# Twelve score pairs in an FFN tile instead of eight, with ten buffers for exponentials and a third residual tile

## The chip, the cores and the metric

The kernel runs on one core of one Trainium2 chip. The metric is device time in microseconds (us) from the first to the last instruction, as the median of several runs; the profile is one further execution with the hardware profiler on. TensorE (PE in the profile) does matmuls, ScalarE (ACT) the exponentials and copies, VectorE (DVE) elementwise work, transposes of 32 x 32 blocks and sums, GpSimd (POOL) casts and adds, SyncE (SP) issues the DMAs.

## The reference

A transformer block on 2048 tokens of width 576, all in float32: pre-normalised multi-query attention with 32 query heads of width 18 that share one key and one value head, then a gated FFN of width 4608 without a nonlinearity.

```python
q = (x @ wq).reshape(B, S, H, Dh).transpose(0, 2, 1, 3)   # S 2048, H 32, Dh 18
k, v = x @ wk, x @ wv
p = softmax(einsum("bhqd,bkd->bhqk", q, k) * Dh ** -0.5)
A = einsum("bhqk,bkd->bhqd", p, v).transpose(0, 2, 1, 3).reshape(B, S, H * Dh) @ wo
h = x0 + A                       # x is layernorm(x0)
n = layernorm(h)
out = h + ((n @ w_gate) * (n @ w_up)) @ w_down
```

## The kernel before, in words

Tokens are worked on in four blocks of 512 (`NB`). Attention of a block goes through 8 groups of four heads (`NG`), each through 16 steps of 128 keys (`NT`). A step is two **pairs**: `pair()` takes a PSUM tile `s` of two banks (two such tiles exist), a buffer `P` for the exponentials (`p_tile`), runs two score matmuls (`scores`, line 596) and one exponential of 128 x 1024 (line 597) from `s` into `P`. So there are 4 x 8 x 16 x 2 = 1024 pairs. `flush()` later turns complete steps into **values** (line 601): four matmuls of 32 columns (two instructions each), which accumulate over the 16 steps of a group in one PSUM bank, `acc`, of which there is one. At a group's end `flush` has VectorE transpose the bank into `os` (line 612). `normalise` divides by the sums and spreads the heads into `ob`; `chunk` and `project` multiply them by `wo` and add the result to the residual `h`. These run from a list, `aux`, of which `run_aux` takes one or two entries in a tile's middle and at its end.

The FFN of a block, `ffn(b)`, has 36 **tiles** of 128 hidden units (`NF`). A tile is 27 steps j of two matmuls each (gate and up, lines 990), then the gate is copied by ScalarE (`g`, line 1020), multiplied by the up half on VectorE (`hf`, line 1024) and made ready for the down product by `left_first` and `left` in odd tiles and `left_sums` in the next even tile (casts on ScalarE, differences on VectorE, line 88 and 89). From the third tile on, every even tile ends with the down product of the two tiles before, `down`, 14 stages of three matmuls (line 950), whose results VectorE adds to `h`, or ScalarE copies to `tmp` (line 957) and GpSimd adds (line 958).

Attention runs ahead inside the FFN: while `more(b + 2)` holds, tiles of block b issue a pair ahead of every fourth step (j = 0, 4, ... 24), and one more after the gate copy: eight in a tile. After `hf` and `left` the tile flushes all its steps at once: this is the tile's **visit** to the values. While pairs run, the gate and up halves use the banks `f` (`pg`, `pu`), otherwise the tile of `s` (`gu`). The last tile of a block has no pairs.

The order on every engine is written out by hand (a manual schedule); semaphores follow from it. Buffers are pools of a fixed number of rooms: a write into a room waits for the last reader of what was there. The exponentials have 6 rooms, from pair 240 on 7. Gate and up weights are loaded into `wr` (two rooms, `load_w`), split into high and low parts by GpSimd and VectorE (`split_w`, at j = 3 of the tile before their use). Residual tiles `h` have two rooms; block b + 2's is loaded at the end of block b's FFN.

Of the kernel before, what the change touches and what calls it, by code (L numbers as in the profile page):

```python
# [17 lines left out]
F32 = mybir.dt.float32  # L18
# [7 lines left out]
P = 128  # L26
# [28 lines left out]
class Block:  # L55
# [509 lines left out]

    def p_tile(self, shape, name):

        i = self.p_next = (self.p_next + 1) % (P_BUFS + (self.p2 is not None and self.n_pair >= P2_FROM))
        pool, tag = (self.pp, "P") if i < P_BUFS else (self.p2, "P2")
        return pool.tile(shape, F32, tag=tag, name=name)  # L570

    def more(self, b):
# [31 lines left out]
    def flush(self, n):  # L604

        for b, g, t, Ps in self.pend[:n]:
            if t == 0:
                self.acc = self.ps_a(f"acc{b}_{g}")
            self.values(self.acc, Ps, t)
            if t == NT - 1:  # L610
                os_ = self.os[g] = self.op.tile([P, TB], F32, tag="os", bufs=1, name=f"os{b}_{g}")
                self.dve.transpose(os_, self.acc)
                if b == 0 and g == NG - 1:
                    self.normalise(b, g, os_)
                else:
                    self.aux.insert(len(self.aux) if b else 0, (self.round + 1, lambda b=b, g=g, o=os_: self.normalise(b, g, o), None))
        del self.pend[:n]

    def run_aux(self, limit=1, within=False):
# [78 lines left out]
    def chunk_of(self, b, c):  # L698
        to = self.heads_to(b, c)
        (self.split_tail if b and c == 4 else self.split)(*to, self.ob[0:rows(b, c), c])  # L700


    def load_wo(self, c):
# [12 lines left out]

    def load_wo_0(self, c):

        r = self.wo_r0[c] = self.w0.tile([P, D], F32, tag="wo_r", bufs=3, name=f"wo_r{c}")
        self.sp.dma_start(r, self.wo0[:, c])  # L720

    def split_wo_0(self):

        self.wo_0 = self.wp.tile([P, 2, 5, D], F32R, tag="X", bufs=1, name="wo_0")
        for c in range(3):
            if c not in self.wo_r0:
                self.load_wo_0(c)
        for c in range(5):
            self.split(self.wo_0[:, 0, c], self.wo_0[:, 1, c], self.wo_r0.pop(c), self.nc.gpsimd.tensor_copy)
            self.wo_in.add(c)  # L730
            if 0 < c < 3:
                self.load_wo_0(c + 2)
            yield
            if c == 2:
                yield
# [114 lines left out]
    def load_w(self, n):  # L850

        if n < NF * NB:
            r = self.wr[n] = self.wp.tile([P, 9, P], F32, tag="wr", bufs=2, name=f"wr{n}")
            self.sp.dma_start(r, self.wgu[n % NF])

    def split_w(self, n):
        if n < NF * NB:
            r = self.wr.pop(n)
            w = self.ws[n] = self.wp.tile([P, 2, 9, P], F32R, tag="ws", bufs=2, name=f"ws{n}")
            self.split(w[:, 0], w[:, 1], r, self.nc.gpsimd.tensor_copy)  # L860
            self.load_w(n + 2)

    def load_wd(self, n):

# [31 lines left out]
    def down(self, b, pair):  # L896

        pe, dve, act, sp, pool = self.pe, self.dve, self.act, self.sp, self.nc.gpsimd
        h = self.h[b]
        W = [self.wdo.pop((b, pair, j), None) for j in range(7)]  # L900
        if pair == NC - 1:
            ys = {}

            def part(s, n, i):

                ms = [(self.A[:, k, 2 * i + s // 2], W[(1, 0, 2, 3)[2 * i + n]][:, l]) for k, l in ((0, 0), (0, 1), (1, 0))]
                for j, (m, k) in enumerate(ms):
                    pe.matmul(ys[s, n][:, :HD], m[:, s % 2 * P:(s % 2 + 1) * P], k, start=(i == j == 0), stop=(i == 1 and j == 2))  # L908

            if b == NB - 1:  # L910
                e = self.ps_s("ye")
                for k, y in enumerate((e[:, 0], e[:, 1], self.ps_f("ye2"), self.ps_f("ye3"), self.ps_m("ye4"), self.ps_a("ye5"))):
                    ys[k // 2, k % 2] = y
                    part(k // 2, k % 2, 0)
            def add(s, n):
                hs, y = h[:, s, n * HD:(n + 1) * HD], ys.pop((s, n))[:, :HD]
                if b < NB - 1 and n:
                    z = self.tmp[:, self.n_tmp % 5]
                    self.n_tmp += 1
                    act.copy(z, y)  # L920
                    pool.tensor_tensor(hs, hs, z, ALU.add)
                else:
                    dve.tensor_tensor(hs, hs, y, ALU.add)

            for s in range(NQ):
                for n in range(2):
                    if (s, n) not in ys:
                        if b < NB - 1:
                            ys[s, n] = self.ps_y(2 * s + n, f"y{b}_{pair}_{s}_{n}")
                        else:  # L930
                            e = self.ps_s("ye6") if n == 0 else e
                            ys[s, n] = e[:, n]
                        part(s, n, 0)
                    part(s, n, 1)
                    if b < NB - 1:
                        add(s, n)
                        yield
                if b == NB - 1:
                    for n in range(2):
                        add(s, n)  # L940
                    yield
                sp.dma_start(self.tokens(self.out, b)[:, s], h[:, s, :])
            return
        c, a = self.ps_f(f"y{b}_{pair}_2"), self.ps_f(f"y{b}_{pair}_0")
        banks = [a, self.ps_m(f"y{b}_{pair}_1"), c]
        for i, (t, bank, (x, w), first, (s, n), on_dve) in enumerate(STAGES):
            y = banks[bank]
            ms = [(self.A[:, k, x], W[w][:, l]) for k, l in ((0, 0), (0, 1), (1, 0))]
            for j, (m, k) in enumerate(ms):
                pe.matmul(y[:, :HD], m[:, t * P:(t + 1) * P], k, start=(first and j == 0), stop=(j == 2), skip_group_check=True)  # L950
            hs = h[:, t + 2 * s, n * HD:(n + 1) * HD]
            if on_dve:
                dve.tensor_tensor(hs, hs, y[:, :HD], ALU.add)  # L953
            else:
                z = self.tmp[:, self.n_tmp % 5]
                self.n_tmp += 1
                act.copy(z, y[:, :HD])  # L957
                pool.tensor_tensor(hs, hs, z, ALU.add)  # L958
            yield

    def room(self):
# [2 lines left out]
        self.A = e[:, 0:14 * HT].rearrange("p (k n q) -> p k n q", k=2, n=7)  # L964
        self.o_hl = e[:, 14 * HT:].rearrange("p (k q) -> p k q", k=2)
        self.S = self.hh.tile([P, 4, HT], F32, tag="S", bufs=1, name="S")
        self.tmp = self.hh.tile([P, 5, HD], F32, tag="tmp", bufs=1, name="tmp")
        self.n_tmp = 0

    def ffn(self, b):  # L970
        pe, act, dve = self.pe, self.act, self.dve
        X, hid, todo = self.X, [], None
        for f in range(NF):
# [10 lines left out]
            j = 0  # L984
            for c in range(9):
                for wk, xk in ((0, 0), (0, 1), (1, 0)):
                    if on and not last and j % 4 == 0 and self.more(b + 2):
                        self.pair()
                    for o, ps in ((0, pg), (64, pu)):
                        pe.matmul(ps, w[o:o + 64, wk, c], X[o:o + 64, xk, c], start=(j == 0), stop=(j == 26))  # L990
# [46 lines left out]
        if b + 1 < NB:  # L1037
            both(self.spread(b + 1), self.down(b, *todo))
            self.more_wd(b + 1, WD_BUFS if b == 0 and self.first else 4)
            if b + 2 < NB:  # L1040
                self.load_x(b + 2)
        else:
            drain(self.down(b, *todo))

    def load_x(self, b):
        h = self.h[b] = self.hp.tile([P, NQ, D], F32, tag="h", name=f"h{b}")
        self.sp.dma_start(h, self.tokens(self.x, b))

    def fill(self, time, keep=2):
# [61 lines left out]
    def begin(self, first):  # L1111
# [3 lines left out]
        self.n_wd = 0  # L1115
        self.os, self.h, self.qt, self.normed, self.wr, self.ws, self.wdo, self.wo_r, self.wos = ({} for _ in range(9))
        self.n_pair, self.half, self.pend, self.aux, self.round = 0, [], [], [], 0
        self.p_next, self.wo_r0, self.wo_in, self.yos, self.n_yo, self.due, self.odd = -1, {}, set(), [], 0, 0.0, 0

    def blocks(self):  # L1120

        work = self.split_wo_0()
        next(work)
        self.load_w(0)
        self.load_w(1)
        self.cast = self.dve.tensor_copy
        self.steps(lambda: len(self.wo_in) < 5, work)
        drain(work)
# [23 lines left out]
        if self.first:  # L1152
            self.load_raw(0)
        else:
            self.load_wd(WD_BUFS)
        for b in range(NB):
            self.ffn(b)
        del self.A, self.o_hl, self.S, self.tmp, self.X, self.ob, self.mv

    def run(self):  # L1160
# [3 lines left out]
        self.wd_dram = tc.dram_tile([NC, P, 7, 2, HD], F32, name="wd_dram")  # L1164
        self.m_dram = tc.dram_tile([NB, 2, H, TB], F32, name="m_dram")
        self.known, self.n_mx = [0] * NB, 0
        self.tqs, self.p2 = [], None
        self.begin(True)
        with ExitStack() as st:
            pool = lambda name, bufs, **k: st.enter_context(tc.tile_pool(name=name, bufs=bufs, **k))  # L1170
            cp, self.lp, self.hp = pool("const", 1), pool("ln", 2), pool("resid", 2)
            self.qp, self.pp, self.op, self.otp = pool("q", 2), pool("P", P_BUFS), pool("o", 1), pool("oT", 1)
            self.ps, self.w0 = pool("ps", 1, space=PSUM), pool("w0", 3)
            self.C = cp.tile([P, C_W], F32, name="C")
            self.ident = self.C[:, C_ID:C_ID + P]
            self.kT = cp.tile([P, S], F32R, name="kT")
# [4 lines left out]
            with tc.tile_pool(name="p0q", bufs=1) as self.p0q:  # L1181
# [4 lines left out]
                with tc.tile_pool(name="qb", bufs=2) as self.qb:  # L1186
# [6 lines left out]
                    live, due = True, 0.0  # L1193
                    while live:
                        if self.n_pair >= WO_FROM and not self.wo_r0:
                            for c in range(3):
                                self.load_wo_0(c)
                        self.pair()
                        due += RATE
# [4 lines left out]
                        self.pair()  # L1204
                        self.run_aux(1)
                        self.flush(len(self.pend) - 1)
            self.wp, self.hh, self.p2 = pool("w", 2), pool("hid", 4), pool("P2", 1)
            self.blocks()
            self.guard()

# [11 lines left out]
LANDING = 12  # L1222
WO_FROM = 200
YO = 10
P2_FROM = 240
STAGES = [(0, 0, P1, True, (0, 0), True), (1, 1, P1, True, (0, 0), True), (0, 2, P5, True, (1, 1), False),
          (0, 0, P6, False, (0, 1), True), (1, 1, P6, False, (0, 1), False), (0, 2, P3, False, (0, 1), False),
          (0, 0, P7, False, (1, 1), False), (1, 1, P7, False, (1, 1), True), (1, 2, P5, True, (1, 1), False),
# [123 lines left out]
```

## Time and profile before

| | |
|---|---|
| median of 3 runs | 2287.27 us (2287.25 to 2287.45) |
| span of the profiled execution | 2285.5 us |
| first FFN matmul | 359.8 us into the span |
| mean granted TensorE clock | 1.000 |
| DMA, mean over the span | 134 GB/s |

A row of the profile's groups and lines reads: source line, engine, operation, output<-inputs, their shapes, count | busy us, mean ns of one | idle time of the engine ahead of them and what ended it. A row of the timeline reads: start in us from the span's start, duration in us, engine, line, operation, output<-inputs, shapes, count of merged instructions, and in brackets the idle time ahead of it and its releaser. A row of the windows reads: window, its length, busy time and count of each engine, granted clock, DMA share, GB/s. Ends of matmuls are modelled, their starts are not; the argument goes by starts.

### The profile page before, as it was taken

Reading aid. Unit: us, or ns where it says so; the run is one execution under the profiler, and the core shown is the slowest. Engines: PE = TensorE matmul, PEld = TensorE weight load, DVE = VectorE, ACT = ScalarE, POOL = GpSimd, SP = SyncE. Lnnn points to the kernel's source line nnn. Section 1 sums busy time; section 2 is a strip of 40 time slices with the busy share of each in tenths; the row PEclk is TensorE's granted clock in tenths of the full one; section 3 lists DMA queues with packets and bytes.
Section 4 is the critical chain, followed back from the end, with each engine's and each line's share of the span. In section 5 each row is a group of like instructions: output and inputs, shape, how many; then the busy total and the mean of one; then the engine's idle time right before and its main releaser. Section 6 shows DMA issues by size and latency. Waiting matters only on the chain.

```text
span 2285.5 us, 45923 instructions
## 1 busy us (share of the span) xinstructions
PE 2264.4 (99%) x18114; PEld 1610.0 (70%) x18114; DVE 1183.9 (52%) x2152; ACT 1438.0 (63%) x1877; POOL 683.1 (30%) x856
## 2 busy tenths in 40 slices
PE   8999999999999999999999999999999999999998
PEld 6433345677777667677767777777767788898887
DVE  8332435565656566343434455444444476566565
ACT  5899887777676676767666767667677623232332
POOL 4000002455554444122221222222122233333332
PEclk9999999999999999999999999999999999999999
DMA  5222314444333444633333443643333355655553
GB/s 174 75 79 72 117 30 136 144 143 147 134 123 129 141 159 135 210 114 123 113 113 108 126 129 125 193 126 120 100 120 116 122 172 174 212 172 172 179 185 112
DMA packets 127129, 306.75 MB, mean 134 GB/s; under 512 B 17553, under 2 KB 17681, under 8 KB 126265
## 3 DMA queue, kind: packets, MB, share of 16 engines
q1 hardware_dynamic: 126905, 303.73, 40.6%
q8 instruction: 145, 2.38, 0.4%
q14 instruction: 79, 0.65, 0.1%
HBM read 233.76 MB, written 55.67 MB: 127 GB/s over the span
## 4 chain that ended last, share of the span: by engine, by line
PE 95%; DVE 2%; DMA 1%; ACT 1%; issue 0%; SPq 0%; POOL 0%; DVEq 0%; ACTq 0%; POOLq 0%
PE pg L990 21%; PE acc L601 20%; PE y L950 17%; PE gu L990 13%; PE s L596 12%; PE pu L990 5%; PE yo L754 3%; PE psq L448 2%; PE y L908 1%; DMA X<-X 1%; PE psk L236 0%; DVE XT L89 0%; PE ye L908 0%; DVE bsa L103 0%; ACT P L597 0%
## 5 line engine op out<-in xcount | busy, mean ns | idle before, releaser
L597 ACT ACTIVATE P<-s 128x1024 f32<-128x1024 f32 x1024 | 1025.4, 1027 | 263.6 <-PE s L596 187.1
L990 PE MATMUL pg<-X,ws 64*128 64x512 f32 x2592 | 702.6, 389 | 0.1
L990 PE MATMUL pu<-X,ws 64*128 64x512 f32 x2592 | 702.5, 389 | 0.1
L990 PEld LDWEIGHTS pg<-X,ws 64*128 64x128 f32 x2592 | 479.4, 185 | 69.2 <-issue 1.2
L990 PEld LDWEIGHTS pu<-X,ws 64*128 64x128 f32 x2592 | 477.3, 185 | 15.2 <-DVE h L755 1.0
L601 PE MATMUL acc<-P,V 128*32 128x512 f32 x4096 | 487.9, 598 | 0.0
L596 PE MATMUL s<-q,kT 56*128 56x512 f32 x2048 | 452.6, 421 | 3.6 <-DVE XT L89 1.8
L950 PEld LDWEIGHTS y<-wdo,room 128*128 128x128 f32 x2856 | 386.1, 188 | 47.6 <-issue 44.2
L950 PE MATMUL y<-wdo,room 128*128 128x288 f32 x2856 | 403.6, 300 | 0.1
L957 ACT COPY tmp<-y 128x288 f32<-128x288 f32 x408 | 162.9, 400 | 331.0 <-PE y L950 313.5
L596 PEld LDWEIGHTS s<-q,kT 56*128 56x128 f32 x2048 | 210.4, 184 | 188.7 <-ACT P L597 106.9
L990 PE MATMUL gu<-X,ws 64*128 64x512 f32 x2592 | 301.7, 389 | 0.6 <-DMA X<-X 0.6
L958 POOL TENSOR_TENSOR x<-x,tmp 128x288 f32<-128x288 f32 x204 | 159.1, 808 | 440.7 <-ACT tmp L957 439.8
L601 PEld LDWEIGHTS acc<-P,V 128*32 128x32 f32 x4096 | 113.9, 109 | 241.6 <-issue 230.6
L990 PEld LDWEIGHTS gu<-X,ws 64*128 64x128 f32 x2592 | 250.1, 184 | 46.3 <-issue 4.7
L88 POOL CAST ws<-wr 128x1152 fp32r<-128x1152 f32 x144 | 171.4, 1190 | 321.8 <-PE pu L990 173.5
L958 POOL TENSOR_TENSOR h<-h,tmp 128x288 f32<-128x288 f32 x204 | 159.0, 810 | 345.4 <-ACT tmp L957 345.1
L89 DVE TENSOR_TENSOR ws<-wr,ws 128x1152 fp32r<-128x1152 f32 x144 | 199.8, 1387 | 75.4 <-POOL ws L88 75.4
L1024 DVE TENSOR_TENSOR hf<-pu,g 128x512 f32<-128x512 f32 x96 | 66.3, 691 | 265.3 <-ACT g L1020 258.6
L953 DVE TENSOR_TENSOR x<-x,y 128x288 f32<-128x288 f32 x272 | 117.4, 453 | 145.5 <-PE y L950 145.5
L953 DVE TENSOR_TENSOR h<-h,y 128x288 f32<-128x288 f32 x272 | 118.1, 454 | 112.0 <-PE y L950 108.9
L89 DVE TENSOR_TENSOR room<-S,room 128x1024 fp32r<-128x1024 f32 x68 | 85.5, 1257 | 144.3 <-ACT room L88 144.3
(172 smaller groups left out, 1630.2 us busy)
## 6 DMA issues: line engine op xcount, KB each, us to landing
wdo<-wd_dram SPq DMA_DIRECT2D x369, 288.0 KB
wr<-in_wgu_dram SPq DMA_DIRECT2D x144, 576.0 KB
wd_dram<-wdo SPq DMA_DIRECT2D x123, 288.0 KB
q<-q_dram SPq DMA_DIRECT2D x64, 216.0 KB
raw<-in_wd_dram SPq DMA_DIRECT2D x36, 288.0 KB
q_dram<-qs SPq DMA_DIRECT2D x15, 504.0 KB
X<-X SPq DMA_DIRECT2D x24, 256.0 KB
ob<-ob SPq DMA_DIRECT2D x121, 36.0 KB
```

What stands on the lines that cost most here:

```text
L88: (copy or self.cast)(hi, src)
L89: self.dve.tensor_tensor(lo, src, f32(hi), ALU.subtract)
L596: self.pe.matmul(s_[:, i], self.kT[o:o + 56, t * P:(t + 1) * P], q[o:o + 56, pr], start=True, stop=True)
L597: self.act.activation(p_, s_, AF.Exp, scale=SCALE)
L601: self.pe.matmul(acc[32 * j:32 * j + 32, :], self.V[:, t, :], Ps[j // 2][:, j % 2, :], start=(t == 0), stop=(t == NT - 1), skip_group_chec ...
L754: pe.matmul(y[:, :HD], m, k, start=(i == 0), stop=(i == len(ms) - 1))
L950: pe.matmul(y[:, :HD], m[:, t * P:(t + 1) * P], k, start=(first and j == 0), stop=(j == 2), skip_group_check=True)
L953: dve.tensor_tensor(hs, hs, y[:, :HD], ALU.add)
L957: act.copy(z, y[:, :HD])
L958: pool.tensor_tensor(hs, hs, z, ALU.add)
L990: pe.matmul(ps, w[o:o + 64, wk, c], X[o:o + 64, xk, c], start=(j == 0), stop=(j == 26))
L1024: dve.tensor_tensor(hf, pu, g, ALU.mult)
```

## The change

- The exponentials get ten rooms: the 6, two in a pool `early` (which holds the raw `wo` chunks first, two at a time instead of three) and two in a pool `late`. All ten are used once the five `wo` chunks are in (`len(self.wo_in) == 5`).
- `SPOTS` replaces every fourth step: eleven places in a tile, and the one after the gate copy as before, so twelve pairs. The visit is still one, at the same place, now for six steps.
- Block 2's residual tile has a room of its own (`hp2`), loaded ahead of block 0's FFN; block 3's is loaded after block 0's.
- To make space, `wr` has one room instead of two (`load_w(n + 1)` after the split of tile n's weights, `load_w(1)` at the start goes) and `tmp` four instead of five.
- `normalise` of a block's first group waits, for blocks 2 and 3, until the block before has its last chunk split out of `ob` (`split_to`).

```diff
@@ p_tile
-        i = self.p_next = (self.p_next + 1) % (P_BUFS + (self.p2 is not None and self.n_pair >= P2_FROM))
-        pool, tag = (self.pp, "P") if i < P_BUFS else (self.p2, "P2")
+        i = self.p_next = (self.p_next + 1) % (P_BUFS + (EARLY + LATE if len(self.wo_in) == 5 else 0))
+        pool, tag = (self.pp, "P") if i < P_BUFS else (self.early, "P2") if i < P_BUFS + EARLY else (self.late, "P3")
@@ flush
-                    self.aux.insert(len(self.aux) if b else 0, (self.round + 1, lambda b=b, g=g, o=os_: self.normalise(b, g, o), None))
+                    free = (lambda b=b: self.split_to >= b) if g == 0 and b > 1 else None
+                    self.aux.insert(len(self.aux) if b else 0, (self.round + 1, lambda b=b, g=g, o=os_: self.normalise(b, g, o), free))
@@ chunk_of
+        if c == 4:
+            self.split_to = b + 1
@@ load_wo_0, split_wo_0
-        r = self.wo_r0[c] = self.w0.tile([P, D], F32, tag="wo_r", bufs=3, name=f"wo_r{c}")
+        r = self.wo_r0[c] = self.early.tile([P, D], F32, tag="P2", name=f"wo_r{c}")
...
-            if 0 < c < 3:
-                self.load_wo_0(c + 2)
+            if c + EARLY < 5:
+                self.load_wo_0(c + EARLY)
@@ load_w, split_w
-            r = self.wr[n] = self.wp.tile([P, 9, P], F32, tag="wr", bufs=2, name=f"wr{n}")
+            r = self.wr[n] = self.wp.tile([P, 9, P], F32, tag="wr", bufs=1, name=f"wr{n}")
...
-            self.load_w(n + 2)
+            self.load_w(n + 1)
@@ down (twice), room
-                    z = self.tmp[:, self.n_tmp % 5]
+                    z = self.tmp[:, self.n_tmp % N_TMP]
...
-        self.tmp = self.hh.tile([P, 5, HD], F32, tag="tmp", bufs=1, name="tmp")
+        self.tmp = self.hh.tile([P, N_TMP, HD], F32, tag="tmp", bufs=1, name="tmp")
@@ ffn
-                    if on and not last and j % 4 == 0 and self.more(b + 2):
+                    if on and not last and j in SPOTS and self.more(b + 2):
                         self.pair()
...
-            if b + 2 < NB:
-                self.load_x(b + 2)
+            if b == 0:
+                self.load_x(3)
@@ load_x
-        h = self.h[b] = self.hp.tile([P, NQ, D], F32, tag="h", name=f"h{b}")
+        pool, tag = (self.hp2, "h2") if b == 2 else (self.hp, "h")
+        h = self.h[b] = pool.tile([P, NQ, D], F32, tag=tag, name=f"h{b}")
@@ blocks
-        self.load_w(1)
...
+        self.load_x(2)
         for b in range(NB):
             self.ffn(b)
@@ run
-            self.ps, self.w0 = pool("ps", 1, space=PSUM), pool("w0", 3)
+            self.ps, self.early = pool("ps", 1, space=PSUM), pool("P2", EARLY)
...
-            self.wp, self.hh, self.p2 = pool("w", 2), pool("hid", 4), pool("P2", 1)
+            self.wp, self.hh, self.late, self.hp2 = pool("w", 2), pool("hid", 4), pool("P3", LATE), pool("resid2", 1)
@@ constants
-P2_FROM = 240
+EARLY, LATE = 2, 2
+N_TMP = 4
+SPOTS = (0, 1, 4, 7, 10, 12, 15, 18, 21, 24, 26)
```

More of the change, by code (lines that the diff above doesn't have):

```diff
@@ L724, in split_wo_0 @@
         self.wo_0 = self.wp.tile([P, 2, 5, D], F32R, tag="X", bufs=1, name="wo_0")
-        for c in range(3):
+        for c in range(EARLY):
             if c not in self.wo_r0:
@@ L954, in down @@
             else:
-                z = self.tmp[:, self.n_tmp % 5]
+                z = self.tmp[:, self.n_tmp % N_TMP]
                 self.n_tmp += 1
@@ L1117, in begin @@
         self.n_pair, self.half, self.pend, self.aux, self.round = 0, [], [], [], 0
-        self.p_next, self.wo_r0, self.wo_in, self.yos, self.n_yo, self.due, self.odd = -1, {}, set(), [], 0, 0.0, 0
+        self.p_next, self.wo_r0, self.wo_in, self.yos, self.n_yo, self.due, self.odd, self.split_to = -1, {}, set(), [], 0, 0.0, 0, 0
     def blocks(self):
@@ L1166, in run @@
         self.known, self.n_mx = [0] * NB, 0
-        self.tqs, self.p2 = [], None
+        self.tqs = []
         self.begin(True)
@@ L1195, in run @@
                         if self.n_pair >= WO_FROM and not self.wo_r0:
-                            for c in range(3):
+                            for c in range(EARLY):
                                 self.load_wo_0(c)
```

## The prediction

> **What bounds the kernel now.** I read the page first: busy shares, slices and chain.
>
> ```profile
> PE 2264.4 (99%) x18114; PEld 1610.0 (70%) x18114; DVE 1183.9 (52%) x2152; ACT 1438.0 (63%) x1877; POOL 683.1 (30%) x856
> ACT  5899887777676676767666767667677623232332
> PE 95%; DVE 2%; DMA 1%; ACT 1%; issue 0%; SPq 0%; POOL 0%; DVEq 0%; ACTq 0%; POOLq 0%
> L597 ACT ACTIVATE P<-s 128x1024 f32<-128x1024 f32 x1024 | 1025.4, 1027 | 263.6 <-PE s L596 187.1
> ```
>
> TensorE is the bound everywhere: 99% busy and 95% of the chain. ScalarE is at six to seven tenths while exponentials run, then at two to three. So a change gains only where it shortens TensorE's own stream, and loses wherever it makes TensorE wait. Next, the groups by line, those of the exponentials up to the first FFN tile (a window that ends at 359.9 us) and those of the gate copies:
>
> ```profile
> L597 ACT ACTIVATE P<-s 128x1024 f32<-128x1024 f32 x272 | 263.4, 1023 | 38.6 <-PE s L596 38.0
> ...
> L1020 ACT COPY g<-pg 128x512 f32<-128x512 f32 x96 | 55.7, 580 | 5.6 <-PE pg L990 5.6
> L1020 ACT COPY g<-gu 128x512 f32<-128x512 f32 x48 | 28.3, 590 | 117.3 <-PE gu L990 117.3
> ```
>
> 272 of the 1024 pairs are done before the FFN, 752 inside it. At eight a tile that is 94 tiles; two more tiles (the last of blocks 0 and 1) use the same banks without pairs, which makes the 96. The other 48 are plain. At twelve a tile the 752 pairs need 62 tiles and one with eight: 35 in block 0 (272 + 420 = 692, under the limit of 768 that `more(2)` sets), 27 and the short one in block 1. So the change can do what it says.
>
> Then the timeline of TensorE, around an odd and an even tile of block 0 and a plain two-tile period of block 3:
>
> ```profile
> 688.31 0.50 PE L596 MATMUL s<-q,kT 56*128 56x512 f32 x2
> ...
> 706.07 0.50 PE L596 MATMUL s<-q,kT 56*128 56x512 f32 x2
> ...
> 707.32 0.41 PE L596 MATMUL s<-q,kT 56*128 56x512 f32 x2
> 707.55 0.39 PE L990 MATMUL pg<-X,ws 64*128 64x512 f32 x1
> ...
> 713.98 0.41 PE L596 MATMUL s<-q,kT 56*128 56x512 f32 x2
> 714.32 3.64 PE L601 MATMUL acc<-P,V 128*32 128x512 f32 x32
> 717.89 0.50 PE L596 MATMUL s<-q,kT 56*128 56x512 f32 x2
> ...
> 725.92 0.39 PE L596 MATMUL s<-q,kT 56*128 56x512 f32 x2
> 726.24 1.06 PE L601 MATMUL acc<-P,V 128*32 128x512 f32 x8
> ...
> 1972.54 0.73 PE L990 MATMUL gu<-X,ws 64*128 64x512 f32 x4
> ...
> 1990.85 0.73 PE L990 MATMUL gu<-X,ws 64*128 64x512 f32 x4
> ```
>
> Even tile (with its down product) 706.07 - 688.31 = 17.76, odd tile 717.89 - 706.07 = 11.82: 29.58 for two tiles with 16 pairs. A plain two tiles take 1990.85 - 1972.54 = 18.31. Sixteen pairs therefore cost 11.27. A score step takes 707.55 - 707.32 = 0.23, and the values of one step (two pairs, 8 instructions) (3.64 - 1.06) / 3 = 0.86.
>
> **What it removes: visits.** A tile with four more pairs and no waiting is longer by 4 x 0.23 + 2 x 0.86 = 2.64. The even tile's last scores come 725.92 - 717.89 = 8.03 after its first, the odd one's 713.98 - 706.07 = 7.91: 0.12 is lost to waiting today. Without it, two tiles of twelve take 29.58 - 0.12 + 5.28 = 34.74. Today the same weights and 24 pairs take 18.31 + 1.5 x 11.27 = 35.22. The gain is 0.48 per two tiles, over 31.3 such periods 15 us. The Trainium skill (TensorEngine Tiling (Array Packing), Key Properties) says that a change of tiling mode drains TensorE, and each visit is such a change, which speaks for the change; the 15 us hold that drain already.
>
> **What it adds, first: ScalarE's pace.** Scores still have two PSUM buffers, so scores i wait until exponential i - 2 has been read. In the program's order FFN matmuls and values stand behind waiting scores on the same engine. The rows of ScalarE:
>
> ```profile
> 348.20 2.85 ACT L597 ACTIVATE P<-s 128x1024 f32<-128x1024 f32 x3
> ...
> 706.61 2.19 ACT L597 ACTIVATE P<-s 128x1024 f32<-128x1024 f32 x2
> 708.69 0.40 ACT L88 CAST room<-hf 128x256 fp32r<-128x256 f32 x1
> 708.99 5.54 ACT L597 ACTIVATE P<-s 128x1024 f32<-128x1024 f32 x5
> 714.43 0.58 ACT L1020 COPY g<-pg 128x512 f32<-128x512 f32 x1
> 715.48 1.02 ACT L597 ACTIVATE P<-s 128x1024 f32<-128x1024 f32 x1 [0.47 <-PE acc L601]
> ...
> 721.71 1.04 ACT L88 CAST room<-S 128x1024 fp32r<-128x1024 f32 x1
> 722.64 2.85 ACT L597 ACTIVATE P<-s 128x1024 f32<-128x1024 f32 x3
> ...
> 849.45 1.03 ACT L597 ACTIVATE P<-s 128x1024 f32<-128x1024 f32 x1
> ...
> 850.53 0.50 PE L596 MATMUL s<-q,kT 56*128 56x512 f32 x2
> ```
>
> The first exponential starts 706.61 - 706.07 = 0.54 after its scores. Back to back, three take 2.85, so one follows another by (2.85 - 1.03) / 2 = 0.91. Scores that wait go 850.53 - (849.45 + 1.03) = 0.05 after the exponential ends. The twelfth scores need the tenth exponential: 0.54 + 9 x 0.91 + 1.03 + 0.05 = 9.81 after the tile's start at the earliest. TensorE alone would be there at 7.91 + 4 x 0.23 = 8.83. It waits 0.98. The new spots, three FFN steps apart, just match 0.91; the two gaps of two steps and the pair after the last matmul do not. Other ScalarE work inside the tile adds in full, since nothing covers it any more: in odd tiles `left_first`, 708.99 - 708.69 = 0.30, in even ones `left_sums`, 722.64 - 721.71 = 0.93. So 1.28 in an odd tile, 1.91 in an even one. There are 30 of each and two block starts without that work: 38 + 57 + 2 = **97 us**. The Trainium skill (ScalarE: Activation LUTs, What ACT_TABLE_LOAD costs) gives an ACTIVATE with immediate operands 186 ns plus 0.833 ns an element, less 93 ns back to back: an estimate of 0.95 for 1024, against 0.91 in this trace. By that page the waiting would be 0.3 longer per tile, about 20 us in all.
>
> **What it adds, second: groups end inside a visit.** 16 steps make a group of heads, which accumulates in one PSUM bank, `acc`. At its end VectorE transposes the bank into `os`, and the next group's values wait for that. 136 steps are done before the FFN, 8 past a group's end. Today's visits of four steps end with every group, so nothing stands behind the transpose for a tile. Visits of six put the ends after 2, 0 and 4 steps in turn. By the tile count, of the 24 group ends in the FFN 15 fall inside a visit: after two steps in 5 odd tiles (1, 9, 17, 25, 33 of block 0) and 3 even (6, 14, 22 of block 1); after four steps in 4 even (6, 14, 22, 30 of block 0) and 3 odd (3, 11, 19 of block 1). Rows of VectorE:
>
> ```profile
> L612 DVE STREAM_TRANSPOSE os<-acc 128x512 f32<-128x512 f32 x24 | 17.2, 718 | 21.4 <-PE acc L601 19.8
> ...
> 93.08 0.72 DVE L612 STREAM_TRANSPOSE os<-acc 128x512 f32<-128x512 f32 x1 [12.61 <-PE acc L601]
> ...
> 94.09 0.64 PE L601 MATMUL acc<-P,V 128*32 128x512 f32 x4
> ...
> 1084.94 0.69 DVE L1024 TENSOR_TENSOR hf<-pu,g 128x512 f32<-128x512 f32 x1 [3.56 <-ACT g L1020]
> ...
> 1087.24 0.68 DVE L89 TENSOR_TENSOR room<-hf,room 128x512 fp32r<-128x512 f32 x1
> ```
>
> In program order `hf`, and in odd tiles `left`, come before the transpose. Count from the visit's start. With ten rooms, exponential 11 waits for the first step's values, as the eighth does today: 715.48 - 714.32 = 1.16. The gate copy is queued behind it, 0.91 later at 2.07, and takes 0.58. `hf` runs from 2.68 to 3.37, the transpose to about 4.1; in odd tiles `left` ends 1087.92 - 1084.94 = 2.98 after `hf` began, at 5.66, the transpose at 6.3. From its end to the next values lies between 0.05 (the wait for ScalarE above) and 0.29 (94.09 - 93.80); I take 0.1, nearest to a wait that really held TensorE. TensorE is ready at 1.72 after two steps, 3.44 after four. It waits 4.7 and 3.0 in odd tiles, 2.5 and 0.8 in even: 5 x 4.7 + 3 x 3.0 + 3 x 2.5 + 4 x 0.8 = **43 us**. Nothing else can hide this: behind `acc` all of TensorE stands.
>
> **What I cost at nothing.**
>
> ```profile
> 702.26 4.80 POOL L958 TENSOR_TENSOR x<-x,tmp 128x288 f32<-128x288 f32 x6 [8.82 <-ACT tmp L957]
> ...
> 704.21 0.40 ACT L957 COPY tmp<-y 128x288 f32<-128x288 f32 x1 [0.40 <-PE y L950]
> ...
> 1975.90 10.01 SPq L854 DMA_DIRECT2D wr<-in_wgu_dram  x2
> ...
> 1984.21 1.35 DVE L89 TENSOR_TENSOR ws<-wr,ws 128x1152 fp32r<-128x1152 f32 x1
> ...
> 1972.50:1990.85 18.35, 18.35 (x153) 16.36 (x152) 11.12 (x20) 5.58 (x12) 6.88 (x9) 1.00 0.52 177
> ...
> PE gu L990 <- DMA X<-X: 0.6, 1, 0.6
> ```
>
> Four `tmp` instead of five: the fifth copy (704.21) needs the first add, done at 702.26 + 0.80 = 703.06; 1.1 to spare, and up to 0.8 a down product if POOL starts late. One `wr` instead of two: SP waits for the same VectorE split as now, so nothing more stands behind it; a load issued at 1975.90, in a plain stretch, now feeds the next split, whose VectorE half comes at 1984.21. 576 KB at the window's 177 GB/s are 3.3 us, the cast 1.2: hidden by 3.8; beyond that each plain tile would be late by the excess. Block 2's residual, 1152 KB, moves ahead of block 0: 6.7 us of DMA behind the raw weights on SP's queue, for data used a block later; nothing to 7 once. Two early loads instead of three: nothing to 3.3 (two of 288 KB), under the steps of pairs. Block 2 now starts without pairs over its X moves; block 3's start lost 0.6 so: +1.
>
> **Sum.** 2285.5 - 15 + 97 + 43 + 1 = 2411.5 for the profiled execution; the median of the runs stands 1.8 above its span: **2413**.
>
> **Rivals.**
> - *ScalarE's pace alone* (the transposes find VectorE free early, or the ends fall elsewhere): without the 43, 2370. For it: VectorE is half idle. Against: `hf` itself hangs on the delayed exponential.
> - *More than both*: the chunk casts of `ob` (0.6) fall inside waiting tiles, and the four `tmp` hold ScalarE for one 0.8 add in each of 31 down products: up to 30 on top, 2443. For it: nothing on ScalarE is covered any more. Against: 1.1 us to spare.
> - *Faster*: the exponentials keep up and only the visits go: 2413 - 97 - 43 = 2273. It decides where an exponential follows another by (8.83 - 0.54 - 1.03 - 0.05) / 9 = 0.80 or less and groups end with visits; the row says 0.91. The skill's drain rule, above, is the argument for it.
> - *It does not do what it says* (pairs stop at the limit and spill into block 2): against it the count above; 2287.
>
> **How the numbers follow.** Forecast 0.6, pace alone 0.18, more than both 0.15, faster 0.04, no change 0.03. The range goes from just under the pace alone (2366) to the third case (2443). A measurement here tells 0.2% from no change, 4.6 us. Faster 0.04, same 0.03, slower 0.93.
>
> **What would show it.** Right: TensorE's waits list scores behind `P` L597 with about a hundred us, and `acc` behind `os` L612 with some forty in 15 places; twelve-pair tiles near 15.8 (odd) and 22.1 (even). Wrong: such tiles near 14.5 and 20.3, or exponentials less than 0.85 apart, or `acc` never late.

## The result, and the profile after

| | before | after |
|---|---|---|
| median of the runs | 2287.36 us (2287.25 to 2287.78) | 2449.62 us (2446.42 to 2452.95) |
| ratio, 95% interval | | 1.0709 [1.0694, 1.0724] |
| span of the profiled execution | 2285.5 us | 2444.6 us |
| mean granted TensorE clock | 1.000 | 0.994 |

The change makes the kernel 7.1% slower. The forecast was 2413 with a range up to 2443: the side is right, and the time lies 6.6 us above the range. First the page of the changed kernel: span, busy shares, the chain by engine and by line, and two groups.

```profile
span 2444.6 us, 45830 instructions
...
PE 2339.9 (96%) x18114; PEld 1572.9 (64%) x18114; DVE 1194.4 (49%) x2152; ACT 1396.7 (57%) x1877; POOL 675.3 (28%) x856
...
PE 62%; ACT 24%; DVE 7%; issue 4%; DMA 1%; SPq 0%; POOL 0%; ACTq 0%; DVEq 0%; POOLq 0%
...
L597 ACT ACTIVATE P<-s 128x1024 f32<-128x1024 f32 x1024 | 982.8, 1045 | 298.9 <-PE s L596 198.2
L601 PE MATMUL acc<-P,V 128*32 128x512 f32 x4096 | 492.6, 606 | 39.3 <-DVE os L612 39.3
```

TensorE has the same 18114 instructions as before, but its share of the chain went from 95% to 62%: ScalarE now holds 24% and VectorE 7%. These are the two engines that TensorE waits for. TensorE's busy time rose too, by 75 us (2264.4 to 2339.9), though the work is the same; some of that is waiting that the modelled ends count as busy, and some is a slower clock, below.

**Scores wait for exponentials.** TensorE's waits in the changed kernel (us in total, times, longest), and its timeline through an odd and an even tile of twelve pairs:

```profile
PE acc L601 <- DVE os L612: 39.3, 15, 4.3
PE s L596 <- ACT P L597: 38.2, 120, 0.9
```

```profile
1613.51 0.50 PE L596 MATMUL s<-q,kT 56*128 56x512 f32 x2
...
1623.70 0.50 PE L596 MATMUL s<-q,kT 56*128 56x512 f32 x2 [0.18 <-ACT P L597]
1624.13 5.36 PE L601 MATMUL acc<-P,V 128*32 128x512 f32 x48
1629.42 0.50 PE L596 MATMUL s<-q,kT 56*128 56x512 f32 x2
...
1635.70 0.50 PE L596 MATMUL s<-q,kT 56*128 56x512 f32 x2 [0.67 <-ACT P L597]
...
1640.28 0.50 PE L596 MATMUL s<-q,kT 56*128 56x512 f32 x2 [0.19 <-ACT P L597]
...
1651.82 0.51 PE L596 MATMUL s<-q,kT 56*128 56x512 f32 x2
```

The last scores start 10.19 after the first in the odd tile and 10.86 in the even one; the prediction had 8.83 + 1.28 = 10.11 and 8.83 + 1.91 = 10.74. The tiles take 15.91 and 22.40 (predicted near 15.8 and 22.1). The row of waits shows only 38.2 us for this, since many waiting scores are put down with no idle time ahead of them. So I took the starts of all score matmuls: first to last of each tile, less what TensorE alone needs (7.91 for eight pairs, 0.23 more for each further one). Summed over the tiles with pairs that is 107.9 us, against 11.6 in the kernel before.

**A group's end inside a visit.** Tile 9 of block 0, in the timelines of TensorE and VectorE:

```profile
548.97 1.92 PE L601 MATMUL acc<-P,V 128*32 128x512 f32 x16
555.23 5.15 PE L601 MATMUL acc<-P,V 128*32 128x512 f32 x32 [4.33 <-DVE os L612]
...
551.66 0.69 DVE L1027 TENSOR_TENSOR hf<-pu,g 128x512 f32<-128x512 f32 x1 [4.66 <-ACT g L1023]
...
553.86 0.69 DVE L89 TENSOR_TENSOR room<-hf,room 128x512 fp32r<-128x512 f32 x1
554.46 0.71 DVE L612 STREAM_TRANSPOSE os<-acc 128x512 f32<-128x512 f32 x1
```

After two steps (16 instructions) TensorE waits 4.33 us. VectorE was idle for 4.66, waiting for the gate copy, and had the transpose queued behind `hf` and `left`. This is the predicted order, and the predicted 15 places: 4.33 where 4.7 was predicted.

**The clock halves after such a wait.** The windows of the changed kernel (window, length, busy time and count of PE, PEld, DVE, ACT, POOL, then the granted clock):

```profile
554.90:558.30 3.40, 3.07 (x16) 0.79 (x20) 1.51 (x2) 0.00 (x0) 2.42 (x3) 0.50 0.35 96
...
1172.73:1176.14 3.41, 1.27 (x12) 0.42 (x16) 3.33 (x6) 0.00 (x0) 0.00 (x0) 1.00 0.00 0
1176.14:1179.55 3.41, 3.41 (x20) 1.84 (x14) 0.00 (x0) 1.41 (x2) 0.00 (x0) 0.50 0.54 173
...
1394.60:1398.01 3.41, 1.47 (x16) 0.55 (x20) 1.31 (x2) 1.47 (x3) 0.00 (x0) 1.00 0.00 0
1398.01:1401.42 3.41, 3.41 (x34) 1.70 (x22) 0.61 (x2) 0.00 (x0) 0.00 (x0) 1.00 0.00 0
```

Right behind the wait of 4.33 TensorE runs at half clock for 3.4 us: 16 to 20 instructions in a window that holds 34 at full clock. The trace has eight such spells ahead of the kernel's end (the kernel before has none): after all five waits of 4.33, after two of the three waits of 2.6, and one at a block's start (2114.8). A spell does half of 3.4 us of work, so it costs 1.7 us; eight cost about 13.6.

**The plain tiles are slower as well.** Tiles 3 to 34 of block 3 have no pairs, the same work in both kernels. (A plain tile here is one without pairs that is not the last of its block; in even tiles it holds the down product.) The windows over that stretch, of the kernel before and of the changed one:

```profile
1972.54:2265.67 293.13, 293.12 (x2401) 258.61 (x2400) 177.14 (x305) 88.88 (x177) 110.66 (x129) 1.00 0.51 173
```

```profile
2127.83:2424.96 297.13, 295.58 (x2401) 258.44 (x2400) 182.90 (x305) 88.88 (x177) 110.97 (x129) 1.00 0.51 172
```

and from the groups by line in it one row each of VectorE and GpSimd, again before and after:

```profile
L887 DVE TENSOR_TENSOR S<-hf,hf 128x256 f32<-128x256 f32 x16 | 6.8, 425 | 0.5
...
L88 POOL CAST ws<-wr 128x1152 fp32r<-128x1152 f32 x32 | 36.9, 1153 | 71.4 <-PE gu L990 71.4
```

```profile
L890 DVE TENSOR_TENSOR S<-hf,hf 128x256 f32<-128x256 f32 x16 | 13.3, 834 | 0.5
...
L88 POOL CAST ws<-wr 128x1152 fp32r<-128x1152 f32 x32 | 37.2, 1162 | 84.9 <-DMA wr<-in_wgu_dram 84.9
```

The stretch takes 4.0 us more, at full clock. GpSimd's cast of the raw weights used to wait for TensorE, now for the load of `wr`. And an addition on VectorE takes twice as long, 834 ns instead of 425. The timelines of one even tile of the changed kernel (GpSimd, VectorE, TensorE), and of one of the kernel before, show how the two hang together:

```profile
1959.07 1.16 POOL L88 CAST ws<-wr 128x1152 fp32r<-128x1152 f32 x1 [5.50 <-DMA wr<-in_wgu_dram]
1959.38 1.11 DVE L890 TENSOR_TENSOR S<-hf,hf 128x256 f32<-128x256 f32 x1
...
1963.89 1.35 DVE L89 TENSOR_TENSOR ws<-wr,ws 128x1152 fp32r<-128x1152 f32 x1
1965.16 0.81 DVE L956 TENSOR_TENSOR h<-h,y 128x288 f32<-128x288 f32 x2
...
1965.66 4.73 PE L953 MATMUL y<-wdo,room 128*128 128x288 f32 x33 [0.22 <-DVE h L956]
```

```profile
1997.33 1.15 POOL L88 CAST ws<-wr 128x1152 fp32r<-128x1152 f32 x1 [4.45 <-PE gu L990]
...
1998.70 0.43 DVE L887 TENSOR_TENSOR S<-hf,hf 128x256 f32<-128x256 f32 x1
...
2002.52 1.35 DVE L89 TENSOR_TENSOR ws<-wr,ws 128x1152 fp32r<-128x1152 f32 x1
```

Before, the cast is over (1998.48) when VectorE starts its addition. After, the cast comes later, because the load does, and lies on top of the addition, which ends 0.26 after the cast (1960.49 and 1960.23). All that is queued behind it on VectorE is 0.7 late: its half of the split, and behind that the sums of the down product, whose PSUM buffers TensorE waits for. The Trainium skill (SBUF — State Buffer, Who interferes with whom) says that a VectorE instruction with two inputs in SBUF contends with a GpSimd instruction that reads SBUF, since they share a pair of ports under an exclusive lock. The trace agrees: 1.11 instead of 0.43, ended 0.26 after the cast.

At the start of blocks 2 and 3 the late load costs TensorE directly. The row of waits of the changed kernel has two entries that the kernel before does not have:

```profile
PE gu L993 <- POOL ws L88: 1.9, 2, 0.9
PE gu L993 <- DVE ws L89: 1.3, 2, 0.7
```

In tile 2 of each of these blocks TensorE waits for both halves of the split itself (from 1768.05 and from 2112.15 on). In block 2 the room comes free at 1758.51, when VectorE has done its half of the split before; the load is issued at 1761.28, behind stores of results and loads of `wdo` on SyncE's queue, and the cast starts at 1767.79. The spell of half clock at 2114.8 follows the waits in block 3.

Tile by tile the span's +159.1 us comes apart like this:

| | predicted | measured |
|---|---|---|
| scores late (107.9 - 11.6); the 97, less 0.12 in 31 periods today | +93 | +96.3 |
| values wait for `os`, 15 places | +43 | +39.3 |
| half clock, seven spells in tiles with pairs | 0 | about +12 |
| plain tiles (excess 21.5 - 2.3, with the spell at 2114.8) | +1 | +19 |
| fewer visits, without those 0.12, and all else (what is left over) | -11 | -7.5 |

The excess of the plain tiles is their time over 6.25 us (odd), 12.06 (even, with its down product) and the output projections in them, summed over all of them. The kernel before has 46 plain tiles, the changed one 77. About 11 us of it lie in the 36 even tiles behind a block's start, 0.3 each, and most of the rest in the first three tiles of blocks 2 and 3. The profiled execution was the quickest of the four; their median stands 3.2 above it.

### The profile page after: what moved, and what is told of

Its sections match the earlier page's. It is cut to its first block, busy times and chain, and to the rows that moved or that the text cites. A ratio compares the mean times of both kernels' runs of the same rounds, so it can differ in the third digit from the quotient of the medians.

```text
span 2444.6 us, 45830 instructions
## 1 busy us (share of the span) xinstructions
PE 2339.9 (96%) x18114; PEld 1572.9 (64%) x18114; DVE 1194.4 (49%) x2152; ACT 1396.7 (57%) x1877; POOL 675.3 (28%) x856
## 4 chain that ended last, share of the span: by engine, by line
PE 62%; ACT 24%; DVE 7%; issue 4%; DMA 1%; SPq 0%; POOL 0%; ACTq 0%; DVEq 0%; POOLq 0%
ACT P L597 21%; PE acc L601 19%; PE y L953 15%; PE gu L993 15%; PE s L596 6%; PE yo L757 3%; ACT room L88 2%; PE psq L448 1%; DVE ws L89 1%; DVE hf L1027 1%; DVE S L890 1%; ACT g L1023 1%; PE pg L993 1%; DVE S L891 1%; DMA wr<-in_wgu_dram 1%
## 5 line engine op out<-in xcount | busy, mean ns | idle before, releaser
L597 ACT ACTIVATE P<-s 128x1024 f32<-128x1024 f32 x1024 | 982.8, 1045 | 298.9 <-PE s L596 198.2
L601 PE MATMUL acc<-P,V 128*32 128x512 f32 x4096 | 492.6, 606 | 39.3 <-DVE os L612 39.3
L993 PE MATMUL pu<-X,ws 64*128 64x512 f32 x1728 | 516.6, 394 | 0.0
L993 PE MATMUL pg<-X,ws 64*128 64x512 f32 x1728 | 515.8, 394 | 0.0
L993 PE MATMUL gu<-X,ws 64*128 64x512 f32 x4320 | 506.2, 390 | 3.5 <-POOL ws L88 1.9
L596 PE MATMUL s<-q,kT 56*128 56x512 f32 x2048 | 465.5, 445 | 41.3 <-ACT P L597 38.2
L993 PEld LDWEIGHTS gu<-X,ws 64*128 64x128 f32 x4320 | 414.8, 185 | 84.9 <-issue 7.4
L596 PEld LDWEIGHTS s<-q,kT 56*128 56x128 f32 x2048 | 195.4, 184 | 327.5 <-ACT P L597 247.0
L993 PEld LDWEIGHTS pg<-X,ws 64*128 64x128 f32 x1728 | 323.0, 187 | 42.8 <-issue 1.0
L961 POOL TENSOR_TENSOR x<-x,tmp 128x288 f32<-128x288 f32 x204 | 159.1, 810 | 647.0 <-ACT tmp L960 646.6
L993 PEld LDWEIGHTS pu<-X,ws 64*128 64x128 f32 x1728 | 322.8, 187 | 6.0 <-DVE h L758 1.3
L1027 DVE TENSOR_TENSOR hf<-pu,g 128x512 f32<-128x512 f32 x64 | 44.3, 692 | 388.3 <-ACT g L1023 388.3
L961 POOL TENSOR_TENSOR h<-h,tmp 128x288 f32<-128x288 f32 x204 | 159.1, 812 | 207.2 <-ACT tmp L960 206.9
L1023 ACT COPY g<-gu 128x512 f32<-128x512 f32 x80 | 47.2, 590 | 199.0 <-PE gu L993 199.0
```

The costliest lines, as they stand in the source:

```text
L596: self.pe.matmul(s_[:, i], self.kT[o:o + 56, t * P:(t + 1) * P], q[o:o + 56, pr], start=True, stop=True)
L597: self.act.activation(p_, s_, AF.Exp, scale=SCALE)
L601: self.pe.matmul(acc[32 * j:32 * j + 32, :], self.V[:, t, :], Ps[j // 2][:, j % 2, :], start=(t == 0), stop=(t == NT - 1), skip_group_chec ...
L1023: act.copy(g, pg)
```

## The experiments

Theory: the first four rows above are the causes, each by itself. The rivals are named with each experiment.

**1. The flush ahead of `hf` and `left`.** The changed kernel; TensorE's order stays, VectorE transposes first.

```diff
@@ ffn, at a tile's end
+            self.flush(len(self.pend))
             hf = ...
             ...
-            self.flush(len(self.pend))
```

> The changed kernel with one move: the visit is issued ahead of hf and left, so that VectorE's transpose of acc stands ahead of them in its queue. Theory (the 39 us that TensorE waits for os come from hf and left being ahead of the transpose, and the eight spells of half clock follow from those waits): each of the 15 waits falls to about 1.0 us, 15 in place of 39; the spells in the FFN blocks with pairs go (12 us); about 2449 - 24 - 12 = 2413. Rival (the transpose waits for something else, as the room of os): the waits stay near 39 us and the time near 2449.

Measured 2421.57 us (2419.9 to 2424.56), ratio 1.0584 [1.0566, 1.0602]. Waits and the timelines of TensorE and VectorE in the same tile 9:

```profile
PE acc L601 <- DVE os L612: 12.6, 15, 0.8
```

```profile
549.65 3.64 PE L601 MATMUL acc<-P,V 128*32 128x512 f32 x32 [0.84 <-DVE os L612]
...
548.88 0.72 DVE L612 STREAM_TRANSPOSE os<-acc 128x512 f32<-128x512 f32 x1 [3.98 <-PE acc L601]
549.58 0.69 DVE L1028 TENSOR_TENSOR hf<-pu,g 128x512 f32<-128x512 f32 x1
```

The waits fall to 0.84 each, every spell of half clock in a tile with pairs is gone (clock 0.999), and the next 32 instructions take 3.64 instead of 5.15. That settles both rows: the transpose stood behind `hf`, and the half clock follows from the wait. The gain is 28 us and not 36: the up half now waits for `hf` in five places (3.8 us in all), the plain tiles lost 25.3 instead of 21.5, and the scores came late by 112.7 instead of 107.9.

**2. The casts of the hidden halves on GpSimd.** The changed kernel; `left_sums` casts on GpSimd in every tile, and `left_first` in the same way.

```diff
-        self.split(self.A[:, 0, 3:7], self.A[:, 1, 3:7], self.S)
+        self.split(self.A[:, 0, 3:7], self.A[:, 1, 3:7], self.S, self.nc.gpsimd.tensor_copy)
```

> The changed kernel with the high casts of left_first and left_sums on GpSimd instead of ScalarE. Theory (scores wait for ScalarE's queue, so that every cast inside a tile adds in full): the twelfth scores come 9.85 after the first in odd and even tiles alike, in place of 10.16 and 10.86; 30 x 0.3 + 30 x 1.0 = 39 us less, about 2410. Rival (scores wait for rooms of P, not for ScalarE's pace): nothing moves, 2449.

Measured 2444.39 us, ratio 1.068 [1.0662, 1.0697]: hardly better than the change. But the scores did what was expected, late by 71.2 us instead of 107.9. Most of what ate it is in the tiles without pairs. TensorE's waits from 1640 us on, changed kernel first, then this one:

```profile
PE y L953 <- DVE h L956: 4.9, 11, 1.2
```

```profile
PE y L953 <- DVE h L956: 27.3, 34, 1.0
```

and one plain tile of this kernel:

```profile
1945.17 1.15 POOL L88 CAST ws<-wr 128x1152 fp32r<-128x1152 f32 x1
...
1945.26 2.14 DVE L89 TENSOR_TENSOR room<-S,room 128x1024 fp32r<-128x1024 f32 x1 [0.94 <-POOL room L88]
```

GpSimd does the new cast first, so the cast of the weights falls on VectorE's subtraction, which takes 2.14 instead of 1.23; the down product's sums are late in nearly every even tile. The clock fell to 0.991, with ten spells of half clock, three of them twice as long: at 1.7 us a step some 8 us more than in the changed kernel. The theory on the scores stands; the time of 2410 that was expected does not, a miss of 34.

**3. One `wr` room in the kernel before,** nothing else: `bufs=1`, `load_w(n + 1)`, no `load_w(1)` at the start.

> The kernel before with one room for wr instead of two and nothing else. Theory (the 20 us that plain tiles lose in the changed kernel come from the single room: the cast waits for its load, the VectorE half comes late and the down product's adds behind it): 46 plain tiles at 0.28 each, about 12 us slower, 2299, with GpSimd waiting for wr and TensorE for h in blocks 2 and 3; tiles with pairs unchanged. Rival (the loss comes from four rooms of tmp, or from pairs ending earlier): within 3 us of 2287.

Measured 2298.46 us (2297.25 to 2298.7), ratio 1.0045 [1.0029, 1.0062]. Its window over tiles 3 to 34 of block 3, and the same VectorE row of the groups in it:

```profile
1979.32:2276.49 297.17, 295.70 (x2401) 260.19 (x2401) 182.99 (x305) 88.80 (x177) 110.58 (x129) 1.00 0.50 172
```

```profile
L887 DVE TENSOR_TENSOR S<-hf,hf 128x256 f32<-128x256 f32 x16 | 14.2, 889 | 0.5
```

297.17 us, as in the changed kernel (297.13), against 293.13. So in this stretch the one room is the cause of the slow tiles, alone and in full. The same waits for the split at block 3's start are there too (0.87 and 0.66, from 1963.66 on), and a spell of half clock behind them (1966.5). The whole kernel is 11 us slower by it.

**4. Eight pairs in the changed kernel.** `SPOTS = (0, 4, 8, 12, 16, 20, 24)`; rooms, residual and the rest stay.

> The changed kernel with the old spots (every fourth step, eight pairs a tile): rooms, residual tile, wr, tmp and early loads stay changed. Theory (all but the single wr of these costs nothing): 2299, as the kernel before with one wr. If the rooms of exponentials or the early residual cost something in the tiles with pairs, it is above that by so much; with the side edits as the main cause it would stay above 2400.

Measured 2303.12 us, ratio 1.0065 [1.0048, 1.0082]. With eight pairs 16 of the change's 162 us are left. It is 4.7 above experiment 3, and most of that shows in the first FFN tiles: GpSimd's second cast of weights in the timeline of experiment 3, then here, and the row of TensorE's waits here that follows from it:

```profile
373.72 1.15 POOL L88 CAST ws<-wr 128x1152 fp32r<-128x1152 f32 x1 [0.93 <-DMA wr<-in_wgu_dram]
```

```profile
378.38 1.15 POOL L88 CAST ws<-wr 128x1152 fp32r<-128x1152 f32 x1 [4.96 <-DMA wr<-in_wgu_dram]
```

```profile
PE pu L993 <- DVE hf L1027: 2.5, 2, 2.2
```

**5. Block 2's residual loaded later,** in tile 6 of block 0 instead of ahead of the FFN, otherwise as experiment 4.

```diff
+                    if j == 21 and b == 0 and f == 6:
+                        self.load_x(2)
 ...
-        self.load_x(2)
```

> The changed kernel with eight evenly spaced pairs in a tile, and the load of block 2's residual tile moved from ahead of block 0's FFN to the 22nd step of its tile 6. Theory: the 4.7 us by which eight pairs in the changed kernel stand above the kernel before with one `wr` room come from that load, which stands ahead of a raw-weight load on SyncE's queue at the FFN's start and makes the first split late (the cast at 378.38 instead of 373.72); moved, the wait of the up half in tile 1 (2.2 us) and the spell of half clock behind it (1.7 us) go: 2299 us, ratio 1.005. Rival: they come from the ten rooms, the four `tmp` or block 2's start: it stays at 2303, ratio 1.007.

Measured 2297.21 us (2294.39 to 2298.83), ratio 1.0048 [1.0032, 1.0065]. The interval overlaps that of experiment 4, so the times alone would not tell; the trace does: the cast starts at 373.17, and the wait of the up half in tile 1 and its spell of half clock are gone. The load ahead of the weights was their cause, at 2.2 + 1.7 = 3.9 us. The times differ by 4 (1.0065 - 1.0048) to 6 (2303.12 - 2297.21). Some of that lies elsewhere: at block 3's start TensorE waits 2.0 for GpSimd's half of the split in the trace of experiment 4 and 1.2 in this one, which the moved load does not explain. In the changed kernel itself it was not taken out; there the same cast is late too (377.27), but TensorE lists no wait of the up half behind `hf`.

**6. Four `tmp` in the kernel before,** nothing else.

> The kernel before with four `tmp` instead of five, nothing else. Theory: the fifth copy finds the first add done with 1.1 us to spare, so nothing changes: 2287 us, ratio 1.000. Rival: where GpSimd starts its adds late, behind a split, ScalarE's copy waits for up to one add of 0.8 us in some of the down products that stand beside pairs (31) and later: 2290 to 2310 us.

Measured 2285.68 us, ratio 0.9998 [0.9988, 1.0007]: no change.

**7. Experiments 1 and 2 together, the casts on GpSimd only while a tile has pairs.**

> The visit ahead of hf as in e1, and the high casts of left_first and left_sums on GpSimd while the tile has pairs, on ScalarE in plain tiles. Theory (ScalarE's pace with every cast in the tile added; e2 gave its gain back in plain tiles only): scores in tiles with pairs come 38 us less late in sum, plain tiles lose as in e1, no half clock beside those that e1 has: 2421.6 - 38 = 2384. Rival (the casts on GpSimd cost as much in tiles with pairs): near 2420.

Measured 2386.41 us, ratio 1.0435 [1.0419, 1.0451]; scores late by 76.8 (112.7 in experiment 1), clock 0.998. Where the collision of experiment 2 is left out, ScalarE's relief comes through: 35 us below experiment 1.

**8. Ten pairs, evenly three steps apart.** Experiment 1 with `SPOTS = (0, 3, 6, 9, 12, 15, 18, 21, 24)`.

> The visit ahead of hf as in e1, with ten pairs a tile, three steps apart and one after the gate copy. Theory (the last scores wait for the exponential two before them at 0.54 + (n - 3) x 0.91 + 1.03 + 0.05 plus the casts): with n = 10 that is 7.99, 8.29 in odd and 8.92 in even tiles, against TensorE's own 8.38: no wait in odd tiles, 0.5 in even ones, 23 us in all in place of 113; 19 group ends inside a visit at 0.84 are 16 us; 69 plain tiles as in e1: about 2330. Rival (the wait goes with the number of pairs, not with the pace): two thirds of e1's loss in tiles with pairs, about 2380.

Measured 2355.41 us, ratio 1.0292 [1.0276, 1.0308]: 25 above the expectation, a miss, and halfway to its rival. The last scores come 8.55 (odd) and 9.25 (even) after the first, where 8.38 and 8.92 were expected; they are late by 50.6 in all, not 23, and that alone is the miss. The prediction's formula for the last scores counts ScalarE's pace alone, and ScalarE keeps it. An even tile's scores show what the formula leaves out:

```profile
636.80 0.50 PE L596 MATMUL s<-q,kT 56*128 56x512 f32 x2
...
642.18 0.49 PE L596 MATMUL s<-q,kT 56*128 56x512 f32 x2 [0.52 <-ACT P L597]
643.22 0.39 PE L596 MATMUL s<-q,kT 56*128 56x512 f32 x2
```

The cast of `left_sums` holds the sixth scores once, to 5.38 after the first. From there TensorE itself needs 0.93 to 1.04 from one pair to the next with three FFN steps between them, more than ScalarE's 0.91, so what it lost there it does not win back. Group ends now fall inside 18 visits and cost 17.2, where 16 were expected.

**9. The kernel before, `left_sums` cast on GpSimd while pairs run.** What experiment 7 gained, without the change: today's even tiles still lose 0.12 to ScalarE.

```diff
-                        self.left_sums()
+                        self.left_sums(self.nc.gpsimd.tensor_copy if on else None)
```

> The kernel before with the high cast of left_sums on GpSimd while the tile has pairs. Theory (the 1.0 us cast makes the last scores of its 47 even tiles 0.19 late on average, 9 us in sum): that goes, about 2279. Rival (GpSimd is late with it and VectorE with the low half, so that hf or the down product waits): no gain, or slower than 2287.

Measured 2280.22 us (2278.89 to 2280.88), ratio 0.9968 [0.9956, 0.9981]. It is 7 us faster than the kernel before, and so than the changed one, and the even tiles' last scores come after 7.91 instead of 8.03.

## Why the prediction was right or wrong

- **The pace of ScalarE: right.** +93 net predicted, +96.3 measured. The pitch is in one row of ScalarE's timeline of the changed kernel:

```profile
1261.98 5.64 ACT L597 ACTIVATE P<-s 128x1024 f32<-128x1024 f32 x6
```

  (5.64 - 1.02) / 5 = 0.92, where 0.91 was taken from a row of before (1.02 is one exponential alone). The estimate by the Trainium skill (ScalarE: Activation LUTs, What ACT_TABLE_LOAD costs), 0.95, would have put 20 us more on the sum; the trace shows the smaller figure. Experiments 2 and 7 confirm that casts on ScalarE add in full: taking them away took 37 and 36 us off the scores' lateness.
- **Group ends inside a visit: right in place and cause,** 39.3 us for 43, in 15 places. The odd tiles were costed at 4.7 and 3.0 and measured 4.33 and 2.6. Experiment 1 shows that it is the order on VectorE and not VectorE's load.
- **"One `wr` room instead of two: hidden by 3.8" is the step that failed.** It asked whether load and cast would be done before VectorE's half of the split as it lies in the kernel before, in a stretch of plain tiles, and answered from there. It did not ask where on GpSimd's and VectorE's queues the cast would then lie, nor how long the load takes at a block's start. The load takes longer than the 3.3 us of the estimate. From the timelines of SyncE and GpSimd in the changed kernel:

```profile
1973.77 0.33 SPq L857 DMA_DIRECT2D wr<-in_wgu_dram  x1
...
1978.38 1.24 POOL L88 CAST ws<-wr 128x1152 fp32r<-128x1152 f32 x1 [6.03 <-DMA wr<-in_wgu_dram]
```

  It is 4.6 from issue to cast. In the stretch of plain tiles the split still reaches TensorE in time; but the late cast runs into VectorE's additions, and the down product, which has nothing to do with these weights, pays. At the start of blocks 2 and 3 the split was late itself. The step named a price ("each plain tile would be late by the excess") and then put it at zero. Measured: 19 us with 77 plain tiles. Experiment 3 shows both parts with the one room alone.
- **A term was missing: the clock.** The sum took TensorE's rate as constant through every wait. All five waits of 4.33 us and two of the three of 2.6 brought half clock behind them, some 12 us in tiles with pairs. The profile of before could not show it, since TensorE's longest wait in its FFN is 0.9 us; no rival had it either. Experiment 1 ties it to the waits.
- **Fewer visits: open.** -11 was predicted without the 0.12, and what is left over is -7.5; but that remainder holds every error of the other rows. No run measures the visits alone.
- **The small ones.** Four `tmp` at nothing: right in the kernel before (experiment 6); in the changed kernel ScalarE's copies wait 20.1 us for GpSimd's adds in 24 places, where before they waited 16.0 in 19. Block 2's residual, "nothing to 7 once": the sum took nothing; 3.9 us in the trace where it was moved, with eight pairs (experiment 5). The two early loads at nothing were not tried alone.

Nineteen and 12 us are nearly all of the 33 by which the span went past the sum. The rival "more than both" named other causes (the casts of `ob`, the four `tmp`) for a like amount; the time came out above it, but not for its reasons: the scores, with every cast among the exponentials in them, are 3 us above the prediction, and the `tmp` waits above rose by 4. The "faster" rival turned on exponentials less than 0.80 apart; they stayed at 0.92.

That two `wr` rooms would bring the changed kernel back by the 19 us was not tried; the second room was given up to make space for the ten.

## What to carry to other kernels

When a buffer is taken away, following its consumer's deadline is not enough: find the instant at which each step of the chain will now run, and look at what is queued behind it there, on engines that have nothing to do with the buffer. When work is packed more densely around the bound engine, what used to be covered (casts, a transpose behind other work, an engine's pace) counts in full; work out the earliest time of each of its instructions before packing. And a wait of TensorE can cost more than its length: here most waits of 2.6 and 4.33 us brought a spell of half clock at 1.7 us behind them, so such a wait is worth splitting or removing first.

## What the runs showed of the hardware

The spells of half clock lie on a grid. In the changed kernel their starts (391.08, 554.92, 722.17, 889.43, 1056.68, 1176.15, 1507.24, 2114.81) are whole multiples of 3.413 us apart, and each lasts one such step. Whether a step is granted half clock goes by TensorE's idle time in the step ahead of it: 3.41 - 1.27 = 2.14 us idle in 1172.73 to 1176.14, half clock after; 3.41 - 1.47 = 1.94 in 1394.60 to 1398.01, full clock after. In all profiles of this case, from the first FFN matmul to the kernel's end, every step with 2.0 us idle or more was followed by half clock, and steps with 1.4 to 1.95 at full clock went either way (1.61 ahead of 2114.8 was, 1.94 was not). Behind a step already at half clock less was enough: experiment 2 has three spells of two steps, in one of which the first step is idle for 0.84. So the same wait of 2.6 us is punished in two tiles and not in a third (1338.5 to 1341.1), which the grid cuts into 1.5 and 1.1. The Trainium skill (TensorE: Matmul & The Clock Gate, What's actually happening) describes a free-running window of 3413 ns and a return to half clock after an idle window. The length and the free running agree with this trace; the condition does not: a step with 1.27 to 1.35 us of matmuls in it is not idle, and was followed by half clock.
